# Sketched attention and a squared-ReLU FFN on one core: another flow for one chunk, and a rearranged prologue

## The chip, the cores and the metric

One Trainium2 chip, one of its cores. The metric is the device time of one execution in microseconds (us), the median over several executions; less is better. The engines of the core are TensorE (PE, matrix products; its weight loads are PEld), VectorE (DVE), ScalarE (ACT), GpSimd (POOL) and SyncE (SP, which only issues DMAs). They run side by side, each through its own list of instructions in order, and wait for one another by semaphores. Matrix products are written to PSUM; the other data lies in SBUF.

## The reference

```python
# q, k, v: (4, 4, 1088, 32)  S1, S2: (8, 32)
def phi(x):
    a = np.einsum('rd,bhsd->bhsr', S1, x)
    b = np.einsum('rd,bhsd->bhsr', S2, x)
    return np.einsum('bhsi,bhsj->bhsij', a, b).reshape(*x.shape[:-1], r * r)
q_p, k_p = (phi(q), phi(k))
kv = np.einsum('bhsf,bhsd->bhfd', k_p, v)
z = np.sum(k_p, axis=2)
num = np.einsum('bhsf,bhfd->bhsd', q_p, kv)
den = np.einsum('bhsf,bhf->bhs', q_p, z)[..., None] + 1e-06
x = (num / den)                    # then (batch, token, 4 heads x 32) -> (4352, 128)
h = np.maximum(x @ w_in, 0.0)      # w_in: 128 x 2048
out = h * h @ w_out                # w_out: 2048 x 128
```

Every token's query and key become 64 features (8 by 8 products of two sketches). Attention is linear: keys and values are summed to a 64 x 32 matrix per head (kv) and a vector of 64 (z), and each query's features are multiplied with them. The quotient goes through a feed-forward net with a squared ReLU. All values are 32-bit floats.

## The kernel before

The work is cut into 4 batches, each batch into 3 chunks of 384, 384 and 320 tokens, and the hidden layer of the FFN into 16 blocks of 128 (`NFF`). One block of one chunk is a step, so there are 192 steps. In a step, `ffn1` multiplies a block of `w_in` (cast to 16 bit) with the chunk's `xT` into a PSUM tile `pg` (two buffers); one engine takes the ReLU (`gt`), one the square (`g2`); `ffn2` multiplies it with `w_o` in 32 bit and adds into the chunk's `po`. `ffn1` runs three steps ahead of `ffn2` (`LA = 3`). As an x is brought to a range that suits 16 bit by a power of two or a per-token scale before the FFN, its square (`beta` or `bt`) is multiplied on at the end.

Attention for the chunks to come runs in between. A small planner (`_Plan`) puts each of its pieces into a step: `P.add(key, engine, cost, needs, function)` takes the first step after those of its needs (two steps after for PE, one for the others, unless `lag` says otherwise) in which the engine's planned load stays under a cap (1.2 us for DVE until the first chunk of batch 1, 5.0 for POOL). `ready` demands that a chunk's x is planned two steps before `ffn1` first reads it. `balance` then chooses for every step which engines take ReLU and square. The instructions are written out in this order and each engine follows it.

There are two flows for a query chunk:

- The transposed flow (all chunks but the first two): `a_qg` (PE, L417) makes the sketches of the queries with features on partitions, in the PSUM tile X; `a_sh` (DVE shuffles, L426) spreads them; `a_qpn` (POOL, L435) multiplies; `a_ndn` (PE, L448) multiplies with `kw` into the PSUM tile N; `a_dT`, `a_rd`, `a_rb`, `a_x` (DVE) divide; `a_ax` (ACT) and `a_sum` (PE, L498) find the size; `a_rs`, `a_s2` (DVE, L513, L504) make powers of two; `a_xs` and `a_beta` (POOL, L522, L531) give `xT` and `bt`. Its output goes through `f_sc` and `f_sT`.
- The old flow (chunks 0 and 1 of batch 0): tokens on partitions after `a_nd` (PE, L576); `a_x1`, `a_x2`, `a_x3` (DVE) divide and scale each token; chunk 0 is then transposed by PE (`a_xp`) and copied by ACT (`a_xT`), chunk 1 by a transposing DMA (`a_xd`). `f_br` (POOL, 16 copies) lays out `beta`; the output goes through `f_oT` and `f_ob` (L770).

X and N exist once each, so who fills them next waits for the last reader: kv of the next batch (`a_kv9`, L314) needs N too, which the plan frees at `s2`.

Before the first step lies a prologue, ordered by hand (L832 to L926). S1 and S2 come by two DMAs on ACT's queue into `s_nat`, are transposed on DVE (`s_T`, L229) and copied into three operands: `sk` (keys), `sr` (three blocks, "replicas" of the query sketches) and `sq`/`sqn`. Keys of batch 0 are transposed (`a_kT`), sketched on PE (`a_kf`), copied by ACT (`a_fs`) and multiplied on DVE (`a_kp`), two or three 128-token tiles at a time; `a_kv` and `a_z` sum them on PE. The three replicas of the query sketches (`replicated`, L847) come first for 128 columns, between the kv steps, then for 256 after them; `products` multiplies them. `keep_warm` (L830) gives PE products of zeros where it would otherwise be idle: 10 at the start (`WARM0`) and 3 before the first FFN step (`WARM`). ACT casts both halves of `w_in`. All loads but S1, S2 and two pieces of v go by SP's queue in the order of the code: k, the first 384 columns of q, v, the rest of q, both halves of `w_in`, both of `w_o`.

Of the kernel before, what the change touches and what calls it, by code (L numbers as in the profile page):

```python
# [23 lines left out]
class _Plan:  # L24
# [5 lines left out]
    def __init__(self, nsteps, cap):  # L30
        self.n, self.cap = nsteps, cap
        self.load = {e: [0.0] * nsteps for e in cap}
        self.at, self.slots = {}, [[] for _ in range(nsteps)]
        self.late = []
# [6 lines left out]
    def add(self, key, eng, dur, needs, f, *args, not_in=(), first=0, lag=None):  # L41
        s = first
        for k in needs:
            s = max(s, self.at[k] + (self.LAG[eng] if lag is None else lag))
        while s < self.n - 1 and (
            (self.load[eng][s] > 0 and self.load[eng][s] + dur > self.cap[eng])
            or s % 16 in not_in
        ):
            s += 1
        self.fix(key, eng, dur, s, f, *args)  # L50
        return s
# [3 lines left out]
def kernel(  # L55
# [26 lines left out]
    WARM0, WARM = 10, 3  # L82
# [3 lines left out]
    KG = [[(0, 2), (2, 2), (4, 2), (6, 3)]]  # L86
# [6 lines left out]
    Square = mybir.ActivationFunctionType.Square  # L93
    Copy = mybir.ActivationFunctionType.Copy
# [14 lines left out]
    def load_qk(dst, src, b, c0, c1):  # L109
        nc.sync.dma_start(  # L110
# [34 lines left out]
    for s_, r0 in ((S1, 0), (S2, 8)):  # L145
        nc.scalar.dma_start(s_nat[r0 : r0 + 8, :], s_[:, :])
# [4 lines left out]
    nc.scalar.copy(zero_a[:, :], zero[:, 0:8])  # L151
# [6 lines left out]
    load_v(vn[0], 0, 2, (nc.scalar, nc.scalar))  # L158
    load_v(vn[0], 0, 1)
    load_qk(qn[0], q, 0, 384, S)  # L160
# [4 lines left out]
    for c in range(2):  # L165
        nc.sync.dma_start(
            w_in32[:, 1024 * c : 1024 * c + 1024], moe_w_in[:, 1024 * c : 1024 * c + 1024]
        )
    for c in range(2):
# [8 lines left out]


    sk = cpool.tile([128, 64], F32)  # L180
    sq = cpool.tile([128, 128], F32)
    nc.gpsimd.memset(sk[:], 0.0)
    nc.gpsimd.memset(sq[:], 0.0)
    sr = cpool.tile([128, 3 * 128], F32)
    nc.gpsimd.memset(sr[:], 0.0)
    kT = cpool.tile([128, SP], F32)
    qT = cpool.tile([128, SP], F32)
    nc.gpsimd.memset(kT[:, S:SP], 0.0)
# [7 lines left out]
    nc.gpsimd.memset(part[:], 2.0**-12)  # L196
    tiny = cpool.tile([128, 1], F32)
# [10 lines left out]
    def a_kT(b, part):  # L208
        if b > 0 and part < 2:
# [4 lines left out]
        elif b > 0:  # L214
            nc.vector.transpose(
                _ap(kq, 0, 128, 256, [[32 * NT, 2], [1, 32]]),
                _ap(kn[b], 0, 128, 1024, [[32, 2], [1, 32]]),
            )
        elif part < 2:
            nc.vector.transpose(  # L220
                _ap(kT, 0, 128, 512 * part, [[32, 4], [128, 4], [1, 32]]),
                _ap(kn[b], 0, 128, 512 * part, [[128, 4], [32, 4], [1, 32]]),
            )
        else:
            nc.vector.transpose(kT[:, 1024:S], kn[b][:, 1024:S])
# [4 lines left out]
    for h in range(H):  # L230
        (nc.vector if h < 2 else nc.gpsimd).tensor_copy(
# [3 lines left out]
    for j_, o_, f_, copy in (  # L235
        (2, 8, [[0, 4], [1, 8]], nc.gpsimd.tensor_copy),
        (1, 4, [[1, 4], [0, 8]], nc.scalar.copy),
        (0, 0, [[1, 4], [0, 8]], nc.gpsimd.tensor_copy),
    ):
# [5 lines left out]
    mask_b = [8 + l % 8 for l in range(32)]  # L245
    mask_a = [[4 * e + l // 8 for l in range(32)] for e in range(E)]
# [44 lines left out]
    def a_kp(b, g):  # L291
        t0, n = KG[b][g]
        fs = st[b, "fs", g]
        kp = wpool.tile([128, 5 * 256], F32, tag="kp", name="kp", bufs=4)
# [11 lines left out]
    def a_kv(b, t):  # L306
        if t == 0:
            st[b, "N"] = psa.tile([128, 1024], F32, tag="N", name="kvp")
            st[b, "kvp"] = st[b, "N"]
        kp, at = st[b, "kp", t] if b == 0 else (st[b, "kp2"], kp2_at(t))  # L310
        n = 64 if b == 0 and t == 8 else 128
# [232 lines left out]
    def a_qc(b, ch, pool=psa, tag="feat"):  # L544
        qc = pool.tile([128, 512], F32, tag=tag, name="qc")
        nc.tensor.matmul(qc[:, 0:384], sq[:, :], qT[:, 384 * ch : 384 * ch + 384])
        st[b, "qc", ch] = qc

    def a_qb(b, ch):
        qb = wpool.tile([128, 384], F32, tag="qb", name="qb")  # L550
        nc.vector.stream_shuffle(in_=st[b, "qc", ch][:, 0:384], out=qb[:, :], mask=mask_b)
        st[b, "qb", ch] = qb

    def a_qa(b, ch, e):
        qa = wpool.tile([128, 384], F32, tag="qa", name="qa")
        nc.vector.stream_shuffle(in_=st[b, "qc", ch][:, 0:384], out=qa[:, :], mask=mask_a[e])
        st[b, "qa", ch, e] = qa

    def a_qp(b, ch, e):
        qp = bpool.tile([128, 384], F32, tag="qp", bufs=4, name="qp")  # L560
        nc.vector.tensor_tensor(
            out=qp[:, :], in0=st[b, "qa", ch, e][:, :], in1=st[b, "qb", ch][:, :], op=mult
        )
        st[b, "qp", ch, e] = qp

    def a_nd(b, t):
        ch, o = t // 3, t % 3
        if o == 0:
            if ch == 0:
                st[b, "nd", ch] = st[b, "N"][:, 512:1024]  # L570
            else:
                st[b, "N"] = psa.tile([128, 1024], F32, tag="N", name="nd")
                st[b, "nd", ch] = st[b, "N"]
        nd = st[b, "nd", ch]
        for e in range(E):
            nc.tensor.matmul(  # L576
                nd[:, 132 * o : 132 * o + 132],
                st[b, "qp", ch, e][:, 128 * o : 128 * o + 128],
                st[b, "kvz"][:, 132 * e : 132 * e + 132],
                start=(e == 0),  # L580
                stop=(e == E - 1),
            )


    def nd_ap(b, ch, off, free):
        return _ap(st[b, "N"], 0, 128, (512 if ch == 0 else 0) + off, free)

    def a_x1(b, ch, o=0, n=3):
        def small(tag, m=4):
            return wpool.tile([128, 3 * m], F32, tag=tag, name=tag)  # L590
        if o == 0:
            st[b, "x1", ch] = tuple(small(x) for x in ("den", "rden", "mx"))
        den, rden, mx = (t_[:, 4 * o : 4 * (o + n)] for t_ in st[b, "x1", ch])
        nc.vector.tensor_scalar(
            out=den, in0=nd_ap(b, ch, 132 * o + 32, [[33, 4 * n]]),
            scalar1=1e-6, scalar2=None, op0=add,
        )
        nc.vector.reciprocal(rden, den)
# [3 lines left out]
        )  # L602

    def a_x2(b, ch):
        def small(tag, m=4):
# [3 lines left out]
        mm, mp, rm = (small(x, 1) for x in ("mm", "mp", "rm"))  # L609
        nc.vector.tensor_tensor(out=m1[:, :], in0=mx[:, :], in1=rden[:, :], op=mult)  # L610
# [5 lines left out]
            out=mp[:, :], in0=mm[:, :], scalar1=1.0 / 1024.0, scalar2=1.0 / 1024.0,  # L616
            op0=mult, op1=add,
        )
        nc.vector.reciprocal(rm[:, :], mp[:, :])
        nc.vector.tensor_tensor(  # L620
            out=_ap(sc, 0, 128, 0, [[4, 3], [1, 4]]),
            in0=_ap(rden, 0, 128, 0, [[4, 3], [1, 4]]),
            in1=_ap(rm, 0, 128, 0, [[1, 3], [0, 4]]),
            op=mult,
        )
        st[b, "x2", ch] = sc, mp

    def a_x3(b, ch, o=0, n=3):
# [5 lines left out]
        sc, mp = st[b, "x2", ch]  # L634
# [6 lines left out]
        if o + n == 3:  # L641
            nc.vector.tensor_tensor(  # L642
                out=st[b, "beta"][:, 3 * ch : 3 * ch + 3], in0=mp[:, :], in1=mp[:, :], op=mult,
# [20 lines left out]
    def a_xd(b, ch):  # L664

        nc.sync.dma_start_transpose(
            _ap(st[b, "xT"], 0, 128, 384 * ch, [[128, 3], [1, 128]]), st[b, "xs", ch][:, :]
        )


# [4 lines left out]
    g2s = {}  # L675

    def ffn1(i, on, cols=None):
# [14 lines left out]
        else:  # L692
            nc.vector.tensor_scalar(  # L693
                out=gt[:, c0:c1], in0=pg[:, c0:c1], scalar1=0.0, scalar2=None, op0=amax
            )
        if on[1] == "ACT":
            nc.scalar.activation(g2[:, c0:c1], gt[:, c0:c1], Square)  # L697
# [37 lines left out]
    def f_br(b, ch):  # L735

        if ch == 0:
            st[b, "br"] = bpool.tile([128, 4 * NT], F32, tag="br", name="br")
        for dm in range(4):
# [86 lines left out]
    def keep_warm(n, cols=512):  # L826

        t_ = st["warm"]
        for _ in range(n):
            nc.tensor.matmul(t_[:, 0:cols], zero[:, 0:128], zero[:, 0:cols])  # L830

    st["warm"] = psf.tile([128, 512], F32, tag="pg", name="warm")  # L832
    keep_warm(WARM0)
    a_kf(0, 0, psf, "pg")
# [5 lines left out]
    a_kf(0, 2, psf, "po")  # L840
    a_kf(0, 3, psf, "po")
# [309 lines left out]
```

## Time and profile before

| what | us |
|---|---|
| median of 8 executions | 196.14 |
| lowest, highest | 195.83, 197.29 |
| the profiled execution (one of the eight) | 197.29 |
| its span, first to last instruction | 195.5 |
| first FFN product of the second layer (`po`, L709) starts | 18.56 |
| second layer L709, 386 matmuls, busy | 145.1 |
| first layer L681, 193 matmuls, busy | 61.6 |
| mean granted clock of TensorE | 0.985 |

How to read the profile: each row names the line of the kernel, the engine, the operation, "out<-in" by the names of the tiles, and a shape. An engine's busy time is its own; PE's is modelled, because matmuls overlap. "PEclk" is the share of the full clock that TensorE was granted, a digit for each fortieth of the span. The chain of work that ended last is followed back from the last instruction: at each step to what released it. Each 32-bit product is two matmul instructions.

### The profile page before, as it was taken

Reading aid. Unit: us, or ns where it says so; the run is one execution under the profiler, and the core shown is the slowest. Engines: PE = TensorE matmul, PEld = TensorE weight load, DVE = VectorE, ACT = ScalarE, POOL = GpSimd, SP = SyncE. Lnnn points to the kernel's source line nnn. Section 1 sums busy time; section 2 is a strip of 40 time slices with the busy share of each in tenths; the row PEclk is TensorE's granted clock in tenths of the full one; section 3 lists DMA queues with packets and bytes.
Section 4 is the critical chain, followed back from the end, with each engine's and each line's share of the span. In section 5 each row is a group of like instructions: output and inputs, shape, how many; then the busy total and the mean of one; then the engine's idle time right before and its main releaser. Section 6 shows DMA issues by size and latency. Waiting matters only on the chain.

```text
span 195.5 us, 4446 instructions
## 1 busy us (share of the span) xinstructions
PE 186.9 (96%) x1639; PEld 113.5 (58%) x1639; DVE 131.4 (67%) x326; ACT 141.7 (72%) x322; POOL 97.6 (50%) x162
## 2 busy tenths in 40 slices
PE   7997999989999999999999999999999999999990
PEld 2873665546566555565566554565566555556990
DVE  2966865995596678855676668865766655567740
ACT  3436886985796977877696987867687968767740
POOL 4844526993193756960473656960483942610000
PEclk9999799999999999999999999999999999999997
DMA  6799420020028420020047320020020110110201
GB/s 190 209 277 268 96 84 20 5 32 12 0 37 214 135 34 3 0 45 0 2 60 210 118 33 3 0 44 0 0 44 2 19 19 0 20 21 0 40 3 34
DMA packets 27199, 11.40 MB, mean 58 GB/s; under 512 B 19178, under 2 KB 25770, under 8 KB 27178
## 3 DMA queue, kind: packets, MB, share of 16 engines
q1 hardware_dynamic: 26726, 11.02, 23.0%
q8 instruction: 13, 0.21, 0.5%
q10 hardware_dynamic: 452, 0.10, 0.2%
q14 instruction: 8, 0.07, 0.1%
HBM read 8.78 MB, written 2.23 MB: 56 GB/s over the span
## 4 chain that ended last, share of the span: by engine, by line
PE 88%; DVE 7%; ACT 1%; issue 1%; DVEq 0%
PE po L709 54%; PE pg L681 15%; PE ndn L448 4%; PE kvp L314 3%; PE warm L830 2%; PE pt L726 2%; PE qg L417 1%; PE rep L847 1%; DVE sh L426 1%; PE kf L258 1%; PE kvp L328 1%; PE kf L357 1%; PE kvp L576 1%; DVE ob L770 1%; PE sm L498 1%; PE nd L576 1%
## 5 line engine op out<-in xcount | busy, mean ns | idle before, releaser
L709 PE MATMUL po<-g,w_o 128*128 128x384 f32 (+3 forms) x386 | 145.1, 462 | 0.0
L697 ACT ACTIVATE g<-gt 128x384 f32<-128x384 f32 (+1 forms) x159 | 79.9, 506 | 21.3 <-DVE gt L693 17.6
L709 PEld LDWEIGHTS po<-g,w_o 128*128 128x128 f32 x386 | 66.8, 192 | 32.7 <-issue 22.4
L691 ACT ACTIVATE gt<-pg 128x384 f32<-128x384 f32 (+2 forms) x124 | 56.4, 458 | 14.9 <-PE pg L681 14.2
L681 PE MATMUL pg<-xT,w_in 128*128 128x384 f16 (+2 forms) x193 | 61.6, 320 | 0.6 <-ACT xT L660 0.2
L693 DVE TENSOR_SCALAR gt<-pg 128x384 f32<-128x384 f32 (+1 forms) x69 | 36.7, 532 | 26.5 <-PE pg L681 25.4
L699 POOL TENSOR_TENSOR g<-gt 128x384 f32<-128x384 f32 (+1 forms) x31 | 23.9, 776 | 48.5 <-ACT gt L691 48.2
L681 PEld LDWEIGHTS <-w_in 128*128 128x128 f16 x193 | 19.0, 98 | 24.6 <-issue 7.5
L435 POOL TENSOR_TENSOR qp<-sh 128x384 f32<-128x384 f32 (+1 forms) x20 | 19.2, 964 | 7.3 <-DVE sh L426 5.1
L426 DVE STREAM_SHUFFLE sh<-qg 128x384 f32<-128x384 f32 (+1 forms) x40 | 21.4, 561 | 0.0
L458 DVE STREAM_TRANSPOSE dT<-ndn 128x384 f32<-128x384 f32 (+1 forms) x10 | 5.4, 544 | 11.3 <-PE ndn L448 11.3
L284 POOL TENSOR_TENSOR kp<-fs 128x1152 f32<-128x1152 f32 x3 | 9.5, 3166 | 5.3 <-DVE fs L277 5.3
L522 POOL TENSOR_TENSOR xT<-x,rs 128x384 f16<-128x384 f32 (+1 forms) x10 | 9.5, 949 | 1.7 <-DVE rs L513 1.7
L741 POOL COPY br<-beta 32x3 f32<-32x3 f32 x32 | 6.5, 203 | 5.6 <-DVE beta L642 4.3
L448 PE MATMUL ndn<-qp,kw 64*32 64x192 f32 (+1 forms) x320 | 8.4, 318 | 0.0
L531 POOL TENSOR_TENSOR bt<-s 128x384 f32<-128x384 f32 (+1 forms) x10 | 7.8, 785 | 0.9 <-DVE s L504 0.9
L448 PEld LDWEIGHTS ndn<-qp,kw 64*32 64x32 f32 x320 | 4.7, 106 | 5.2 <-issue 3.8
L340 POOL TENSOR_TENSOR ks<-kp 128x1024 f32<-128x1024 f32 x3 | 7.1, 2370 | 0.2
L513 DVE TENSOR_SCALAR rs<-sm 128x384 uint32<-128x384 uint32 (+1 forms) x10 | 5.2, 521 | 2.5 <-PE sm L498 2.5
L314 PE MATMUL kvp<-kp,vn 128*32 128x64 f32 (+1 forms) x288 | 5.9, 221 | 0.7 <-DVE s L504 0.7
L351 POOL TENSOR_TENSOR ks<-ks 128x512 f32<-128x512 f32 (+1 forms) x6 | 6.2, 1035 | 0.5
L314 PEld LDWEIGHTS kvp<-kp,vn 128*32 128x32 f32 (+1 forms) x288 | 4.7, 109 | 2.8 <-DVE s L504 1.3
(119 smaller groups left out, 157.4 us busy)
## 6 DMA issues: line engine op xcount, KB each, us to landing
vn<-in_v_dram SPq DMA_DIRECT2D x32, 64.0 KB, 3.9
kn<-in_k_dram SPq DMA_DIRECT2D x3, 544.0 KB, 12.2
qn<-in_q_dram SPq DMA_DIRECT2D x3, 544.0 KB, 3.3
out_dram<-oT SPq DMA_DIRECT2D x24, 48.0 KB, 1.9
w_in<-in_moe_w_in_dram SPq DMA_DIRECT2D x2, 512.0 KB, 5.3
w_o<-in_moe_w_out_dram SPq DMA_DIRECT2D x2, 512.0 KB, 11.0
out_dram<-oT SPq DMA_DIRECT2D x12, 40.0 KB, 1.7
out_dram<-ob SPq DMA_DIRECT2D x8, 48.0 KB, 1.9
```

The source lines that it names most:

```text
L284: (nc.vector if g == 0 else nc.gpsimd).tensor_tensor(out=_ap(st[b, "kp2"], 0, 128, 128 * NT * g, [[64, 2 * NT], [8, 8], [1, 8]]), in0=_ap( ...
L314: nc.tensor.matmul(st[b, "kvp"][32 * h : 32 * h + 32, 0:64], _ap(vn[b], 0, n, v0 + dv * h, [[1, 32]]), kp[0:n, at[h] : at[h] + 64], start= ...
L426: nc.vector.stream_shuffle(in_=_ap(st[b, "qg", ch], 0, 128, 0, [[512, 2], [1, n]]), out=_ap(t_, 0, 128, 0, [[n, 2], [1, n]]), mask=mask_q[ ...
L435: nc.gpsimd.tensor_tensor(out=qp[:, 0 : 2 * n], in0=st[b, "sh", ch, s, 0][:, 0 : 2 * n], in1=st[b, "sh", ch, s, 1][:, 0 : 2 * n], op=mult,)
L448: nc.tensor.matmul(nd[32 * h : 32 * h + 32, 512 * g + 192 * i : 512 * g + 192 * i + n], st[b, "kw"][64 * g : 64 * g + 64, 128 * i + 32 * h ...
L522: nc.gpsimd.tensor_tensor(out=st[b, "xT"][:, 384 * ch : 384 * ch + n], in0=st[b, "x", ch][:, 0:n], in1=st[b, "rs", ch][:, 0:n], op=mult,)
L681: nc.tensor.matmul(pg[:, c0:c1], w_in[:, 128 * c : 128 * c + 128], st[b, "xT"][:, 384 * ch + c0 : 384 * ch + c1],)
L691: nc.scalar.activation(gt[:, c0:c1], pg[:, c0:c1], Relu)
L693: nc.vector.tensor_scalar(out=gt[:, c0:c1], in0=pg[:, c0:c1], scalar1=0.0, scalar2=None, op0=amax)
L697: nc.scalar.activation(g2[:, c0:c1], gt[:, c0:c1], Square)
L699: (nc.vector if on[1] == "DVE" else nc.gpsimd).tensor_tensor(out=g2[:, c0:c1], in0=gt[:, c0:c1], in1=gt[:, c0:c1], op=mult)
L709: nc.tensor.matmul(st["po", b, ch][:, c0:c1], w_o[:, 128 * c : 128 * c + 128], g2s[i][1][:, c0:c1], start=first, stop=(c == NFF - 1), skip ...
```

## The change

It moves chunk 1 of batch 0 to the transposed flow and rearranges the prologue:

- `old_chunk` and its helpers (`a_qc`, `a_qb`, `a_qa`, `a_qp`, `a_nd`, `a_xd`) go. Chunk 1 of batch 0 now runs through `feature_tasks`, `nd_tasks` and `x_tasks`; its sketches `a_qg(0, 1)`, the transposes `a_kvT(0)` and the copy `a_kw(0)` stand in the prologue, the first two while DVE works on the token scale of chunk 0.
- S2 is loaded by a DMA on GpSimd's queue, before its memsets. The v pieces of ACT's queue go to SP. q comes in three pieces, `w_in` and `w_o` in alternating halves.
- Key tiles 4 to 8 are sketched by eight products with features on partitions (`kf4`), turned by one DVE transpose (`fs4`), and multiplied in two parts. The kv sums of batch 0 lie in a `po` buffer.
- Replicas are made for all 384 columns: blocks 2 and 0 before all kv steps, block 1 after them.
- In `a_x1` the `den` of chunk 0 goes to ACT; `a_x2` uses a power of two by bit operations, one DVE instruction less. `beta` needs one more after xs.
- The second half of `w_in` is cast by POOL in two pieces. Four of the 16 `f_br` copies of chunk 0 stay ahead of the steps, twelve are planned.
- Two of the four `sk` copies go from POOL to ACT. `WARM0` is 8 and a half one, `WARM` 5.
- A square on ACT is written after the next step's ReLU (`square_due`), except in the last chunk.
- The planner treats POOL as one sequence of work with measured lengths; the costs of `balance` are computed from widths.

```diff
+        if eng == "POOL":
+            d, t = dur / 0.85, float(s)
+            for t0, t1 in sorted(self.pool):
+                if t + d <= t0:
+                    break
+                t = max(t, t1)
+            self.pool.append((t, t + d))
+            s = int(t)
+            self.fix(key, eng, dur, s, f, *args)
+            self.at[key] = max(s, int(t + d - 0.6))
+            return s
...
-    for s_, r0 in ((S1, 0), (S2, 8)):
-        nc.scalar.dma_start(s_nat[r0 : r0 + 8, :], s_[:, :])
+    nc.gpsimd.dma_start(s_nat[8:16, :], S2[:, :])
+    nc.scalar.dma_start(s_nat[0:8, :], S1[:, :])
...
+    load_qk(qn[0], q, 0, 384, 768)
+    load_w_in(0, nc.sync)
+    load_w_o(0)
+    load_qk(qn[0], q, 0, 768, S)
+    load_w_in(1, nc.sync)
+    load_w_o(1)
...
-        (nc.vector if h < 2 else nc.gpsimd).tensor_copy(
+        (nc.vector.tensor_copy if h < 2 else nc.scalar.copy)(
...
+        if ch == 0:
+            nc.scalar.activation(
+                den, nd_ap(b, ch, 132 * o + 32, [[33, 4 * n]]), Iden, bias=eps[:, 0:1]
+            )
...
+    def square_due():
+        while due:
+            dst, src = due.pop()
+            nc.scalar.activation(dst, src, Square)
...
+        square_due()
         if on[1] == "ACT":
-            nc.scalar.activation(g2[:, c0:c1], gt[:, c0:c1], Square)
+            due.append((g2[:, c0:c1], gt[:, c0:c1]))
+            if i >= NS - NFF:
+                square_due()
...
-    a_kf(0, 2, psf, "po")
-    a_kf(0, 3, psf, "po")
+    a_sr(1, nc.scalar.copy)
+    kf4 = psa.tile([128, 1024], F32, tag="N", name="kf")
+    for g in range(2):
+        for p0 in range(4):
+            nc.tensor.matmul(
+                kf4[32 * p0 : 32 * p0 + 32, 512 * g : 512 * g + 160],
+                sk[64 * g : 64 * g + 64, 32 * g : 32 * g + 32],
+                kq[64 * g : 64 * g + 64, 32 * NT * p0 + 128 : 32 * NT * p0 + 288],
+            )
     a_qT(0, 0, 384)
...
-    replicated(2, 0, 128, psf, "pg")
+    replicated(2, psf.tile([128, 512], F32, tag="pg", name="rep"))
+    x0 = psa.tile([128, 1024], F32, tag="X", name="rep")
+    replicated(0, x0[:, 0:512])
     a_kp(0, 0)
     a_kp(0, 1)
+    fs4 = wpool.tile([128, 320], F32, tag="fs", name="fs")
+    nc.vector.transpose(
+        _ap(fs4, 0, 128, 0, [[32, 2], [64, 5], [1, 32]]),
+        _ap(kf4, 0, 128, 0, [[512, 2], [32, 5], [1, 32]]),
+    )
+    kp4 = wpool.tile([128, 5 * 256], F32, tag="kp", name="kp", bufs=3)
+    for lo, n in ((0, 2), (2, 3)):
+        nc.vector.tensor_tensor(
...
-    nc.scalar.copy(qb[:, 0:128], rep[2, 0][:, 0:128])
-    products(0, 128)
-    replicated(2, 128, 384, psf, "pg")
-    replicated(0, 128, 384, psf, "po")
-    replicated(1, 128, 384, psf, "po")
+    nc.scalar.copy(qb[:, :], rep[2][:, 0:384])
+    products(0)
+    replicated(1, x0[:, 512:1024])
     a_kvz(0)
-    nc.scalar.copy(qb[:, 128:384], rep[2, 128][:, 0:256])
-    products(128, 384)
+    products(1)
+    a_qT(0, 384, 768)
     a_kvs(0)
...
+    a_kvT(0)
+    a_qg(0, 1)
     st["warm"] = psf.tile([128, 512], F32, tag="pg", name="warm")
     keep_warm(WARM)
     a_x1(0, 0)
+    w_cast(0, 1024, nc.scalar.copy)
     a_x2(0, 0)
...
     a_xT(0, 0, 1, 2)
-    a_qb(0, 1)
-    f_br(0, 0)
+    a_kw(0)
...
-    old_chunk()
+    P.at["kw", 0] = -1
+    feature_tasks(0, 1)
+    P.add(("qT", 0, 2), "DVE", 0.45, [], a_qT, 0, 768, S)
+    f_br(0, 0, 0, 1)
+    for i in range(2):
+        P.add(("w", i), "POOL", 0.6, [], w_cast, 1024 + 512 * i, 512, nc.gpsimd.tensor_copy)
+    assert P.at["w", 1] < 5
+    P.add(("br", 0, 0), "POOL", 2.6, [], f_br, 0, 0, 1, 4)
+    nd_tasks(0, 1)
+    x_tasks(0, 1)
     feature_tasks(0, 2)
```

## The prediction

> **What bounds the kernel now.** I read the page first, then the chain of work that ended last in order of time, then the waits of PE, then PE's timeline step by step, and last the one-microsecond windows of the start. The page:
>
> ```profile
> span 195.5 us, 4446 instructions
> PE 186.9 (96%) x1639; PEld 113.5 (58%) x1639; DVE 131.4 (67%) x326; ACT 141.7 (72%) x322; POOL 97.6 (50%) x162
> PEclk9999799999999999999999999999999999999997
> PE 88%; DVE 7%; ACT 1%; issue 1%; DVEq 0%
> ```
>
> PE is the bound, and 88% of the chain is PE. Only what shortens PE's work, lets it start earlier or removes a stall can count. The chain shows where PE was not the one waited for:
>
> ```profile
> 10.92 1.49 PE rep L847 x6
> 12.42 1.50 PE kvp L576 x12
> 15.93 0.62 DVE xs L635 x2
> 17.07 0.55 ACT xT L660 x2
> 18.72 1.36 PE po L709 x4
> ...
> 36.11 1.15 DVE de L467
> ...
> 39.91 1.47 DVE ob L770
> ...
> 43.73 1.21 PE kvp L314 x72
> 45.44 0.65 PE po L709 x2
> ```
>
> Up to 18.6 us a serial prologue runs. From 45.3 us on, the chain is PE without a break: the second product's start-to-start is 0.81 us for 384 columns and 0.67 us for 320, plus PE's own attention tasks. Between lies one weak place, 39.4 to 45.3 us. PE's timeline there (start, duration):
>
> ```profile
> 39.35 0.81 PE L709 MATMUL po<-g,w_o 128*128 128x384 f32 x2
> 40.33 0.81 PE L709 MATMUL po<-g,w_o 128*128 128x384 f32 x2
> 41.26 0.81 PE L709 MATMUL po<-g,w_o 128*128 128x384 f32 x2
> 42.20 0.81 PE L709 MATMUL po<-g,w_o 128*128 128x384 f32 x2
> 45.27 0.81 PE L709 MATMUL po<-g,w_o 128*128 128x384 f32 x2
> ```
>
> Two steps take 0.93 and 0.94 us, and the last gap is 3.07 us, where the same gap (kv of the next batch inside) is 2.28 us at 85.28 and at 129.19. So 2 x 0.125 + 0.79 = 1.04 us is stall. Its cause:
>
> ```profile
> PE kvp L314 <- DVE s L504: 0.7, 1, 0.7
> ```
>
> kv of batch 1 waits for the accumulator N, which VectorE's s2 of chunk (0,2) frees late. The start has a second loss (columns: busy time of each engine, then PEclk):
>
> ```profile
> 16.00:17.00 1.00, 0.19 (x3) 0.28 (x4) 1.00 (x5) 0.00 (x0) 0.28 (x2) 1.00 1.05 335
> 19.00:20.00 1.00, 1.00 (x3) 0.63 (x4) 0.22 (x1) 0.75 (x2) 0.84 (x5) 0.50 0.84 158
> ```
>
> PE is nearly idle at 16 us, and about 3.4 us of half clock follow (18.8 to 22.2 us). The first three steps take 1.95, 1.60 and 0.86 us, 4.41 against 3 x 0.81 = 2.42: 1.99 us lost to clock and start-up together.
>
> **What the skill says.** The Trainium skill, "TensorE: Matmul & The Clock Gate", Part 1, says the array clock is halved after a window of about 3.4 us with too little work, and that the windows run free of the kernel. The 3.4 us at 0.50 agree; the threshold is not shown here. "SBUF — State Buffer", section Who interferes with whom, says GpSimd and VectorE lock each other out of a shared port pair. The trace agrees: `de` on ten elements takes 1.14 us at 36.11 beside a 3.12 us GpSimd product, against 0.17 us for `den` on twelve at 14.02. "DMA: Bandwidth & Descriptors", Specifications, gives about 1 us to the first byte from the GpSimd queue and 0.6 us from the others; no GpSimd DMA is in this trace.
>
> **The change, prologue.** S2 alone on the GpSimd queue: by the trace both S transfers have landed at 4.27 us, and `s_T` starts at 4.40, just after the kT transpose (3.59 + 0.71 = 4.30). Above, the gain is at most 0.1 us. Below, if the GpSimd transfer lands at 5.3, everything after it moves 1 us. Issued at about 0.95 (after the memset of `s_nat`), with the page's 1 us to the first byte and the 0.9 us from first packet to landing that S1 shows (2.53 to 3.47), it lands at an estimated 2.9, so 1.4 us of slack: I take 0. The GpSimd memsets queued behind it (1.9 us, 0.74 to 2.65) then end near 4, before `s_T`.
>
> The key path. VectorE does transposes and the first two kp to about 7.55 (start-to-start 0.61 for 512 elements, first at 6.3). New there is the fs4 transpose (0.45 us; fs L277 of 288 elements has 0.43) in place of four ScalarE copies, then kp4 in parts of 512 and 768: done at 7.55 + 0.45 + 0.61 + 0.94 = 9.55, where the last kp ended at 9.08. On PE two full replicas (0.64 us each) stand before kv. The second needs GpSimd's sr block 0, at about 7.0 (two sk copies, 0.43 us, leave the queue ahead of the eight sr copies that ended at 8.28, and four of these eight no longer precede block 0 under VectorE's lock). So kv starts at 7.8, not 7.66. That 0.15 us is covered by kp4, which kv 6 to 8 wait for; without that cover it would be 0.15 to 0.7. kv 6 to 8 run at 9.62, 9.84 and 10.06, and `kvt` can start at 10.56 rather than 10.99: 0.43 us earlier.
>
> After kv, before has six replica matmuls (1.49 us) before `nd`; now one replica (0.64), with the first product on VectorE already done. kvz ends at 11.41, `nd` runs 11.5 to 12.95 (12 matmuls, 1.34 us to the last start), and the token scale can start at 13.1 rather than 14.02: 0.92. Its own chain loses two VectorE instructions: `den` goes to ScalarE beside the reduce and `mp` goes, at about 0.2 us each (14.02, 14.23; 15.31, 15.51). xs then starts at 14.6 rather than 15.93: 1.3 us. The kv transposes, qg and five warm-up matmuls (0.22 us each) fill PE meanwhile to about 14.7; qc (0.88) and its shuffle are gone.
>
> On ScalarE the kw copy (0.37 us) now stands between xT and the first relu: minus 0.3. So po starts at 17.5 rather than 18.56. The second step hangs on a ScalarE square that moves behind relu 2 and ends 0.66 us earlier than its 19.36. I take 0.85 as the mean; ends 0 and 1.3.
>
> **The loop.** Removed from PE in batch 0: nd of chunk 1 (0.90 + 0.45 in steps at 22.97 and 24.68) and kvT (0.21) = 1.56. Added: ndn with qg (2.02 - 0.81 = 1.21, the step at 49.53) and the sum (0.17) = 1.38. Gain 0.18. Removed from VectorE for this chunk: two qa, two qp, x1 to x3, about 5 us; added about as much (four sh, dT, rd, rb, x, rs, s2). The chunk's transposing DMA, SP's wait for it and GpSimd's sixteen br copies (3.56 us) go; GpSimd gets two products, xs, bt and two weight casts.
>
> The plan by hand: sh in steps 0 and 1, nd in 4, sum in 9, rs in 10, xs in 11; it is due when step 13 opens. From the sum to that opening are 3 x 0.81 = 2.43 us, for sum, rs (0.5), xs (0.95) and three hops of about 0.15: slack about 0.4. Kv of batch 1 moves from step 22 to about 30, by which time N (s2 in step 23) is long free, so the 0.79 us goes. The two ScalarE-bound steps also go: a relu and its own square are 0.50 apart and the next relu 0.43 later (37.33, 37.83, 38.26); with the square one step late both spacings can be 0.43, 0.86 a step for 0.93. Of 1.04 I take back 0.84 and leave 0.2 for new waits, which next would come at chunk 1's xs. Later steps have no stall to lose, and their PE tasks are the same; the new costs of the planner count 0 there.
>
> **Sum.** 0.85 + 0.18 + 0.84 = 1.87 us. The profiled execution took 197.29 us (195.5 span and 1.8 around it) and would take 195.4. It is 1.15 us above the median of 196.14; how much of that is the half-clock window is not shown. Against the median: 194.3.
>
> **Rivals.** (1) The half clock goes too: the gap before the first ffn matmul is filled by two more warm-ups and less waiting. Against it, about 2.5 us of thin work between 15 and 17.5 remain, as now. Of the 1.99 us start-up loss about 1.4 would go: 192.9. (2) The front gives nothing, because S2 or a replica is late (1 us), and a new wait takes the old stall's place: only 0.2 is left, 195.9. For it: an unseen queue, and kv behind two replicas. Against: each has cover above. (3) Slower: chunk 1 starves PE at step 13. Its chain, from shuffles to xs, alternates VectorE, GpSimd, PE and ScalarE in 11 steps; the old one had until a transposing DMA at 28.54 landed about 31, with 2.7 us to spare. Each VectorE instruction caught behind GpSimd costs about 1 us (`de` 1.14, `ob` 1.64 at 39.80), and GpSimd waits in its queue for the second half of w_in before the products. From 2.5 us over the slack it decides; three such blocks and no slack give 2.7: 197.0. Against: hand start-to-starts put xs at about 29 us, PE's need at about 30.
>
> **Numbers.** 194.3 has chance 0.66, with its own range 193.5 to 195.4; rival 1 0.12, rival 2 0.10, rival 3 0.12. Counting 0.3% (0.6 us) as what a measurement tells from none: faster 0.78, same 0.10, slower 0.12. The range, 192.9 to 196.1, leaves rival 3 and the far edges out.
>
> **What would show it.** First po near 17.5 us and xs near 14.6; kvt near 10.6; `s_T` still at 4.4; kv of batch 1 without a wait on s2; no PE gap at the first matmul of chunk 1; the loop's later steps at 0.81 and 0.67 as now. I am wrong if `s_T` starts after 5, if PE waits on xT (0,1) for over a microsecond, or if ScalarE sets the first twelve steps.

## The result, and the profile after

The changed kernel took 197.23 us (median of 20 executions, 195.5 to 199.12) beside 195.9 us for the kernel before (57 executions): slower by 1.3 us, where 194.3 us was forecast. The ratio is 1.0033 with the interval [1.0013, 1.0053]; ratios here leave out executions more than 1.5% above the fastest of the same kernel, medians count them all. Executions of the changed kernel stand in three groups, near 195.5, 197.1 and 199.1 us, while those of before lie between 195.4 and 196.6 us with five exceptions. The execution profiled before (197.29 us) was such an exception, with a half-clock window at 18.8 us; the one profiled after took 199.16 us.

The page of after (span, busy time of PE, shares of the chain):

```profile
span 197.4 us, 4576 instructions
...
PE 188.0 (95%) x1675; PEld 111.7 (57%) x1675; DVE 121.4 (62%) x303; ACT 139.4 (71%) x342; POOL 96.3 (49%) x144
...
PE 86%; DVE 7%; ACT 2%; DMA 2%; issue 1%; DVEq 0%; ACTq 0%
```

VectorE has ten microseconds less to do than before, and PE is the bound as it was. New in the chain's shares is DMA. The chain of after in order of time (start, length, what):

```profile
1.25 3.45 DMA s_nat<-in_S_dram
5.61 1.94 PE kf L276 x8
7.55 0.71 PE kf L839 x16
8.27 2.86 PE rep L849 x4
15.43 1.59 PE nd L910 x12
...
40.56 2.57 DVE ob L764
...
52.03 1.14 PE kvp L334 x72
```

Three things are to be seen. S2's transfer, issued on the GpSimd queue at 1.25 us, opens the chain. Two replicas, forecast at 0.64 us each, hold PE from 8.27 to 11.1 us, and `nd` starts at 15.43 us instead of the forecast 11.5. And a stall by `ob` stands at 40.56 us, where the stall before kv of batch 1 has gone: that group starts at 51.96 us right behind its step, and its gap between two second products is 2.25 us (51.22 to 53.47), as at the later batches.

PE's timeline of after tells why the front is late (start, busy time of the group, idle before it and its releaser in brackets):

```profile
1.23 3.81 PE L824 MATMUL warm<-zero 128*128 128x512 f16 x9 [1.23 <-DVE zero L161]
5.61 1.94 PE L276 MATMUL kf<-sk,kT 128*128 128x64 f32 x8 [0.57 <-ACT sk L251]
...
12.98 0.44 PE L348 MATMUL kvp<-kp,ones 128*32 128x64 f32 x8
13.19 0.38 PE L334 MATMUL kvp<-kp,vn 128*32 128x64 f32 x8
13.40 0.28 PE L348 MATMUL kvp<-kp,ones 128*32 128x64 f32 x8
13.51 0.28 PE L334 MATMUL kvp<-kp,vn 128*32 128x64 f32 x8
```

The same groups of eight start 0.21 us apart up to 13.4 us and 0.11 us apart after it: PE ran at half clock until then. The throttle's first record in this trace is full clock from 13.38 us; ahead of that record the PEclk column shows 1.00, which is no reading. In the trace of before, whose first warm-ups take 0.43 us each for 0.22 later on, that record is at 5.14 us. So after stays at half clock for 8.2 us more, with its front up to the kv sums in them, behind a gap of 0.57 us that before does not have. PE's timeline of before at that place:

```profile
1.23 4.25 PE L830 MATMUL warm<-zero 128*128 128x512 f16 x10 [1.23 <-DVE zero L149]
5.31 2.14 PE L258 MATMUL kf<-sk,kT 128*128 128x64 f32 x18
```

The stall at 40 us, from after's list of PE's waits and the timelines of VectorE and GpSimd:

```profile
PE sm L518 <- ACT ax L513: 0.7, 1, 0.7
```

```profile
40.34 0.22 DVE L491 RECIPROCAL rd<-de 128x10 f32<-128x10 f32 x1
40.48 2.65 DVE L764 TENSOR_TENSOR ob<-oT,br 128x384 f32<-128x384 f32 x1
43.05 0.50 DVE L496 STREAM_TRANSPOSE rb<-rd 128x320 f32<-128x320 f32 x1
43.59 0.49 DVE L503 TENSOR_TENSOR x<-ndn,rb 128x320 f32<-128x320 f32 x1
```

```profile
40.36 2.36 POOL L360 TENSOR_TENSOR ks<-kp 128x1024 f32<-128x1024 f32 x1
```

GpSimd's `ks1` starts 0.12 us ahead of `ob` and runs to 42.72 us; `ob`, two inputs from SBUF, takes 2.65 us. The token scale of chunk (0,2), which hangs behind it in VectorE's queue (`rb`, `x`, then `ax` on ScalarE), is late, and the sum that PE has next waits.

### The profile page after: what moved, and what is told of

It is laid out like the page before. It is cut to its first block, busy times and chain, and to the rows that moved or that the text cites. A ratio compares the mean times of both kernels' runs of the same rounds, so it can differ in the third digit from the quotient of the medians.

```text
span 197.4 us, 4576 instructions
## 1 busy us (share of the span) xinstructions
PE 188.0 (95%) x1675; PEld 111.7 (57%) x1675; DVE 121.4 (62%) x303; ACT 139.4 (71%) x342; POOL 96.3 (49%) x144
## 4 chain that ended last, share of the span: by engine, by line
PE 86%; DVE 7%; ACT 2%; DMA 2%; issue 1%; DVEq 0%; ACTq 0%
PE po L703 54%; PE pg L672 14%; PE ndn L468 4%; PE kvp L334 3%; PE pt L720 2%; DMA s_nat<-in_S_dram 2%; PE qg L437 2%; PE rep L849 1%; DVE ob L764 1%; PE kvp L348 1%; PE kf L276 1%; PE nd L910 1%; PE sm L518 1%; PE kf L377 1%; ACT g L666 1%
## 5 line engine op out<-in xcount | busy, mean ns | idle before, releaser
L682 ACT ACTIVATE gt<-pg 128x384 f32<-128x384 f32 (+2 forms) x143 | 67.3, 475 | 28.3 <-PE pg L672 27.6
L703 PEld LDWEIGHTS po<-g,w_o 128*128 128x128 f32 x386 | 65.8, 190 | 33.8 <-ACT g L666 19.3
L684 DVE TENSOR_SCALAR gt<-pg 128x384 f32<-128x384 f32 (+1 forms) x50 | 26.1, 523 | 30.9 <-PE pg L672 24.3
L693 POOL TENSOR_TENSOR g<-gt 128x320 f32<-128x320 f32 (+1 forms) x28 | 21.5, 774 | 45.5 <-ACT gt L682 45.4
L455 POOL TENSOR_TENSOR qp<-sh 128x384 f32<-128x384 f32 (+1 forms) x22 | 20.9, 952 | 12.0 <-DVE sh L446 12.0
L446 DVE STREAM_SHUFFLE sh<-qg 128x384 f32<-128x384 f32 (+1 forms) x44 | 22.4, 565 | 0.0
L735 POOL COPY br<-beta 32x3 f32<-32x3 f32 x16 | 2.9, 183 | 9.6 <-DMA vn<-in_v_dram 8.9
L513 ACT ACTIVATE ax<-x,tiny 128x384 bf16<-128x384 f32 (+1 forms) x11 | 6.5, 590 | 1.3 <-DVE x L503 1.3
L749 DVE SCALAR_TENSOR_TENSOR sc<-po,bt 128x384 f32<-128x384 f32 (+1 forms) x10 | 5.3, 532 | 3.3 <-PE po L703 3.1
L334 PEld LDWEIGHTS kvp<-kp,vn 128*32 128x32 f32 x288 | 5.4, 120 | 2.7 <-issue 1.6
```

Of the source, the lines that this page charges most:

```text
L334: nc.tensor.matmul(st[b, "kvp"][32 * h : 32 * h + 32, 0:64], _ap(vn[b], 0, n, v0 + dv * h, [[1, 32]]), kp[0:n, at[h] : at[h] + 64], start= ...
L446: nc.vector.stream_shuffle(in_=_ap(st[b, "qg", ch], 0, 128, 0, [[512, 2], [1, n]]), out=_ap(t_, 0, 128, 0, [[n, 2], [1, n]]), mask=mask_q[ ...
L455: nc.gpsimd.tensor_tensor(out=qp[:, 0 : 2 * n], in0=st[b, "sh", ch, s, 0][:, 0 : 2 * n], in1=st[b, "sh", ch, s, 1][:, 0 : 2 * n], op=mult,)
L682: nc.scalar.activation(gt[:, c0:c1], pg[:, c0:c1], Relu)
L684: nc.vector.tensor_scalar(out=gt[:, c0:c1], in0=pg[:, c0:c1], scalar1=0.0, scalar2=None, op0=amax)
L693: (nc.vector if on[1] == "DVE" else nc.gpsimd).tensor_tensor(out=g2[:, c0:c1], in0=gt[:, c0:c1], in1=gt[:, c0:c1], op=mult)
```

## The experiments

Theory A was: S2 lands late, PE idles before the key sketches, and the half clock lasts longer. B: the new order of the prologue is itself slower or brings the groups of times. C: new stalls in the loop. After the first four runs A split into theory W (too little PE work ahead of the key sketches, the count of warm-ups) and the price of S2 itself. Ratios are to the kernel before, on the same chip. The last column counts from 196.7 us because the changed kernel's groups part there; in e7 and e9 to e15, whose fastest executions take 193.3 to 194.2 us, it counts only those some 2.5 us or more above the fastest.

| kernel | median us (executions) | ratio, interval | at 196.7 us or over |
|---|---|---|---|
| e1 change again | 197.25 (20) | 1.0030 [1.0004, 1.0056] | 15 |
| e2 change, S2 on ScalarE's queue | 196.97 (22) | 1.0023 [1.0003, 1.0042] | 15 |
| e3 change, ten warm-ups | 196.22 (22) | 1.0022 [1.0007, 1.0037] | 7 |
| e4 before, S2 on GpSimd's queue | 196.13 (22) | 1.0018 [1.0009, 1.0027] | 1 |
| e5 before, eight warm-ups | 199.33 (4) | 1.0163 [1.0131, 1.0195] | 4 |
| e6 start repaired (e2 and e3) | 196.03 (22) | 1.0002 [0.9983, 1.0021] | 5 |
| e7 e6, `ob` two steps later | 194.75 (13) | 0.9935 [0.9914, 0.9957] | 0 |
| e8 e6, `den` on VectorE, transposes moved | 198.04 (17) | 1.0051 [1.0022, 1.0081] | 14 |
| e9 e7, three warm-ups before the scale | 194.84 (10) | 0.9944 [0.9912, 0.9975] | 0 |
| e10 e7, first warm-ups split | 195.25 (22) | 0.9954 [0.9932, 0.9975] | 7 |
| e11 e7, `den` on VectorE, own tile | 193.88 (6) | 0.9903 [0.9869, 0.9937] | 0 |
| e12 e9 and e11 | 194.08 (19) | 0.9920 [0.9896, 0.9945] | 0 |
| e13 e11, S2 on GpSimd's queue | 194.98 (14) | 0.9939 [0.9917, 0.9961] | 1 |
| e14 e11, eight warm-ups | 194.22 (13) | 0.9919 [0.9894, 0.9944] | 3 |
| e15 e11 again | 194.44 (8) | 0.9936 [0.9905, 0.9967] | 0 |

Before stood at 195.73 (e1 to e4, 3 of 73 executions at 196.7 or over), 195.83 (e5 to e8, 2 of 45), 195.84 (e9 to e12, 4 of 44) and 195.92 us (e13 to e15, 1 of 28).

### The start: S2 and the warm-ups (e1 to e6)

e1 is the changed kernel unedited.

> The changed kernel once more, for a profile in another phase of the clock's windows. Theory A (S2 lands late from the GpSimd queue, PE idles before the key sketches, and the half clock then lasts one or two windows of 3.4 us longer): times at separate levels near 195.6, 197.2 and 199, and where the level is low, PE is at full clock from about 5 us on. Theory B (the new order of the prologue is slow by itself): the low level too has its first po later than 18 us. Theory C (new stalls in the loop): a stall of over 1 us near chunk 2 of batch 0 in every profile.

```diff
-    nc.gpsimd.dma_start(s_nat[8:16, :], S2[:, :])
     nc.scalar.dma_start(s_nat[0:8, :], S1[:, :])
+    nc.scalar.dma_start(s_nat[8:16, :], S2[:, :])
```

> The changed kernel with S2 back on ScalarE's queue behind S1. Theory A: s_T starts at 4.4 instead of 4.8 us, PE's idle gap before the key sketches shrinks from 0.57 to under 0.2 us, the levels at 197 and 199 go, median 195.0 to 195.4. Theory B or C: the levels stay and the median moves by less than 0.3 us.

```diff
-    WARM0, WARM = 8, 5
+    WARM0, WARM = 10, 5
```

> The changed kernel with 10.5 instead of 8.5 warm-up products ahead of the key sketches. Theory A: s_T still starts at 4.8, but PE has no gap and the level at 199 goes; the lowest time is that of the changed kernel or up to 0.3 us more, the median about 1 us below it. Theory B or C: no difference beyond 0.3 us.

e4 is the kernel before with S2 issued by `nc.gpsimd` ahead of S1, as the change has it.

> The kernel before with S2 alone moved to the GpSimd queue. Theory A: s_T starts at about 4.8 instead of 4.4 us, the key sketches 0.35 us later, PE's gap before them stays under 0.3 us because ten warm-up products end at 5.5, so the time grows by 0.3 to 0.5 us and the level at 199 is rare. Theory B or C: no change over 0.2 us.

e1 repeated the loss and the stall by `ob` (2.65 us at 40.45 us), as C expected. Its profile fell into the group near 199 us, so what A and B say of the lowest group was not seen in it. e2 kept the groups of times, and PE's gap is 0.31 us where under 0.2 was expected (0.30 in e1), so S2's queue does not make the groups, and A as it stood fell.

What the groups are can be read from the throttle's records. Within each trace the changes of the clock lie multiples of 3.41 us apart; one such window at half clock costs a busy PE up to 1.7 us, which is about the spacing of the groups. The execution of after (199.16 us) comes to full clock at 13.38 us and keeps it; that of e1 (199.16 us too) comes to it at 10.09 us and falls back once, from 20.33 to 23.74 us.

With ten warm-ups (e3) PE has no gap before the first key sketch; its timeline of e3:

```profile
1.23 4.66 PE L824 MATMUL warm<-zero 128*128 128x512 f16 x11 [1.23 <-DVE zero L161]
5.68 1.12 PE L276 MATMUL kf<-sk,kT 128*128 128x64 f32 x8
```

The key sketches start 0.07 us later than in after (5.61 us) and take 1.12 us for 1.94; full clock holds from 5.92 us, and the first matmul of the first product starts at 16.80 us instead of 20.11. The median falls by 1.0 us against e1; two executions near 199 us and over are left. e4 prices S2 alone: 0.4 us more than before, `s_T` at 4.62 us instead of 4.40. The number of warm-ups was then taken by itself, in the kernel before:

```diff
-    WARM0, WARM = 10, 3
+    WARM0, WARM = 8, 3
```

> Kernel before with eight warm-up matmuls of 512 columns ahead of the key sketches instead of ten, nothing else. Theory W (too little work in TensorE's first window lets the half clock last longer): PE stands idle some 0.4 us before the first key sketch, some executions fall on levels about 1.5 and 3.5 us higher, as those of the changed kernel do, and the median rises by 0.3 to 1.5 us; in a profile the full clock starts later than 5.1 us or a half-clock window stands later. Rival B (the new order of the prologue itself brings the levels): before stays at 195.7 with nearly all runs within 0.6 us.

PE's timeline of e5:

```profile
1.23 3.60 PE L830 MATMUL warm<-zero 128*128 128x512 f16 x8 [1.23 <-DVE zero L149]
5.36 3.04 PE L258 MATMUL kf<-sk,kT 128*128 128x64 f32 x13 [0.53 <-POOL sk L231]
```

Two warm-ups fewer cost the kernel before 3.5 us, in all four executions: a gap of 0.53 us, key sketches of 3.04 us, and full clock only from 13.89 us, as in after. The new order of the prologue is not needed for that; W holds, and the loss was larger than it expected.

e6 joins the edits of e2 and e3.

> Changed kernel with ten warm-ups and S2 back on the ScalarE queue. Theory W: the levels vanish, all runs within 0.7 us, median near 195.5 (before less 0 to 0.4): the stall in the loop (1.4 us) still eats what the prologue gained. Rival B: the levels of 197 and 199 stay in a third of the runs or more.

The group near 199 us is gone and the change is even with before. W's median (195.5) and spread (0.7 us) were missed: 196.03 us, from 195.27 to 197.26. Five executions remain at 196.7 to 197.3: the profiled one has a half-clock window from 18.26 to 21.68 us, as the one of before had, behind PE's thin stretch before the first product.

### The loop: `ob` behind `ks1` (e7)

```diff
     where = balance()
+    late_ob = next(t_ for t_ in P.slots[18] if t_[0] is f_ob)
+    P.slots[18].remove(late_ob)
+    P.slots[20].append(late_ob)
```

> As the start-repaired kernel, and chunk 0's last product and its store are issued two steps later (step 20 in place of 18), after the token scale of chunk (0,2), with everything else in its place. Theory L (GpSimd's ks1 holds the shared port, the product waits behind it and holds up the sum that PE needs): the 1.4 us gap of PE before that sum goes, and the time falls by 1.0 to 1.4 us against the start-repaired kernel. Rival: the sum waits for its own chain or kv of batch 1 takes the wait over; gain under 0.3 us.

Timelines of e7: VectorE, GpSimd beside its `ob`, then PE:

```profile
37.88 0.22 DVE L491 RECIPROCAL rd<-de 128x10 f32<-128x10 f32 x1
38.13 0.51 DVE L496 STREAM_TRANSPOSE rb<-rd 128x320 f32<-128x320 f32 x1
38.68 0.49 DVE L503 TENSOR_TENSOR x<-ndn,rb 128x320 f32<-128x320 f32 x1
...
40.57 1.18 DVE L764 TENSOR_TENSOR ob<-oT,br 128x384 f32<-128x384 f32 x1
```

```profile
40.34 1.00 POOL L455 TENSOR_TENSOR qp<-sh 128x384 f32<-128x384 f32 x1
```

```profile
40.75 0.81 PE L703 MATMUL po<-g,w_o 128*128 128x384 f32 x2
41.40 0.30 PE L518 MATMUL sm<-ax,part 128*128 128x320 bf16 x1
41.53 0.33 PE L672 MATMUL pg<-xT,w_in 128*128 128x384 f16 x1
41.70 0.81 PE L703 MATMUL po<-g,w_o 128*128 128x384 f32 x2
```

`rb` follows `rd` by 0.25 us instead of 2.71, and the sum runs between two steps without a wait; the step that holds it takes 0.95 us instead of 2.30 (after: 43.22 to 45.52 us). The time falls by 1.28 us against e6, the ratio from 1.0002 to 0.9935, with intervals apart: the place of `ob` made the stall, at the size that theory L expected. That GpSimd is what holds `ob` was not varied by itself, but the times fit it closely: `ob` ends 0.41 us after the GpSimd product that it overlaps, in after (42.72 and 43.13 us), in e6 (40.69, 41.10) and in e7 (41.34, 41.75), though that product takes 2.36 us in the first two and 1.00 us in the last. In e7 PE has no wait that leads back to `ob`.

### The denominator on ScalarE (e8, e11)

What e6 shows of `den` and the reduce (ScalarE's timeline, then VectorE's):

```profile
13.64 0.27 ACT L574 ACTIVATE den<-nd,eps 128x12 f32<-128x12 f32 x1 [2.19 <-PE nd L416]
```

```profile
13.95 0.56 DVE L582 TENSOR_REDUCE mx<-nd 128x12 f32<-128x384 f32 x1 [1.36 <-ACT den L574]
```

`den` waits for L416, the kv transposes that write the same PSUM tile, and `mx` waits for `den`. The Trainium skill, "PSUM — Partial Sum Buffer", section Terms, says that two engines may not be on one PSUM bank and quadrant at once, reads included; both read `nd` there, and the trace shows them one after the other.

```diff
-        if ch == 0:
+        if ch < 0:
             nc.scalar.activation(
...
-    a_kvT(0)
     a_qg(0, 1)
...
     a_x1(0, 0)
+    a_kvT(0)
```

> As the start-repaired kernel, with the denominator of chunk 0 back on VectorE and the transposes of kv emitted behind it. Theory S (ScalarE's denominator does not run beside VectorE's reduce: the reduce waits for it, and it waits for the kv transposes): xs starts 0.3 to 0.6 us earlier than with the start repaired alone, and the time falls by as much. Rival: the reduce is held by nd itself, so xs does not move or moves later by the 0.2 us of the added VectorE instruction.

The edit was badly placed. VectorE's timeline of e8:

```profile
14.67 0.17 DVE L605 SCALAR_TENSOR_TENSOR sc<-rden,rm 128x12 f32<-128x12 f32 x1
16.47 0.62 DVE L620 TENSOR_TENSOR xs<-nd,sc 128x128 f16<-128x128 f32 x2 [1.64 <-PE nd L416]
```

The scale was ready 0.61 us earlier than in e6 (15.28; `nd` itself was 0.10 earlier), but xs then waited 1.64 us for the transposes, which now wrote the tile ahead of it. They came late because PE stood for 1.11 us before them without a releaser ("issue", treated below); another 0.39 us followed behind them, a half-clock window followed at 18.11 us, and 14 of 17 executions stood at 196.7 us or over. e11 gives the transposes a tile of their own instead and leaves them in place, on the base of e7:

```diff
-                st[b, "N"][:, 512 + 128 * i : 640 + 128 * i],
+                st["kvT"][:, 128 * i : 128 * i + 128],
...
+        if b == 0:
+            st["kvT"] = psf.tile([128, 512], F32, tag="po", name="kvT")[:, 0:256]
```

> As the kernel with the late product, with the denominator of chunk 0 on VectorE and the kv transposes in a PSUM tile of their own, in their old place on PE. Theory S (the tile shared with the transposes and the ScalarE denominator hold the reduce): den starts 0.3 us earlier than before, mx 0.5 us, xs 0.4 us earlier counted from kvz; if PE then waits for instructions, xp moves less, 0 to 0.3 us. Rival: xs does not move.

VectorE's timeline of e11, then PE's:

```profile
13.43 0.17 DVE L582 TENSOR_SCALAR den<-nd 128x12 f32<-128x12 f32 x1 [0.77 <-PE nd L914]
13.52 0.55 DVE L586 TENSOR_REDUCE mx<-nd 128x12 f32<-128x384 f32 x1
...
15.05 0.62 DVE L624 TENSOR_TENSOR xs<-nd,sc 128x128 f16<-128x128 f32 x2
```

```profile
15.47 0.59 PE L828 MATMUL warm<-zero 128*128 128x512 f16 x2 [0.61 <-issue]
15.90 0.49 PE L646 MATMUL xp<-iden,xs 128*128 128x128 f16 x3
```

From `kvz` to xs it is 3.82 us (11.23 to 15.05) instead of 4.33 in e6 (11.15 to 15.48): theory S holds, with 0.5 us where 0.4 was expected. e11 moves `den` and gives the transposes their own tile at once; which of the two gives the 0.5 us is not separated. In time, 193.88 us stands beside 194.75 of e7 on another chip, and the intervals overlap; so do those of e9 and e12, which differ by the same edit on one chip (194.84 and 194.08 us). e15, e11's kernel again, gave 194.44. What the 0.5 us is worth in time is therefore not settled, and PE's lines say why it need not show: xp did not start at xs.

### PE without instructions (e9, e10, e12)

In e6, e7 and e11 PE stands for 0.6 to 1.5 us after the third warm-up, and the profile names no releaser ("issue"). In e7 a 16 KB packet of the queue of kind instruction starts at 14.61 us and takes 0.96 us; PE goes on at 16.86, when xs (16.11, 0.62 us) is done. Theory I is that PE had used up what was fetched.

```diff
-    WARM0, WARM = 10, 5
+    WARM0, WARM = 10, 3
```

> As the kernel with the late product (start repaired), with three warm-up matmuls before the token scale instead of five. Theory I (PE runs out of fetched instructions there: a 16 KB packet of its instruction queue starts near 13.4 us, and PE stands without a wait until some 1.4 us after it has come): PE issues the same number of instructions before it stands, so the idle stretch now ends in xp itself, at the moment at which the fourth warm-up ran, and xp starts 0.2 to 0.4 us earlier; time 0 to 0.4 us less. Rival (the fourth warm-up waits for its PSUM buffer or another event, not for instructions): no idle put down to issue is left, xp starts 0.3 us after xs.

```diff
-    keep_warm(WARM0)
+    keep_warm(2 * WARM0, 256)
```

> As the kernel with the late product, with the ten first warm-ups of 512 columns as twenty of 256: the same columns, twenty PE instructions more. Theory I: the idle stretch put down to issue comes about twenty instructions earlier, in the key-value transposes or qg before the third warm-up, and its packet starts some tenths of a microsecond earlier; den, mx and xs move only if the transposes are held. Rival (a hidden event): the stretch stays behind the third warm-up.

PE's timeline of e9, then of e10:

```profile
17.21 0.33 PE L642 MATMUL xp<-iden,xs 128*128 128x128 f16 x3 [1.73 <-DVE beta L632]
```

```profile
13.54 0.53 PE L437 MATMUL qg<-qT,sqn 64*32 64x192 f32 x9
14.31 0.53 PE L437 MATMUL qg<-qT,sqn 64*32 64x192 f32 x7 [0.24 <-issue]
14.76 1.25 PE L824 MATMUL warm<-zero 128*128 128x512 f16 x5
15.90 0.61 PE L642 MATMUL xp<-iden,xs 128*128 128x128 f16 x3
```

In e9 the idle stretch ends in xp, 1.42 us after the packet has come (14.77 + 1.02 = 15.79 us), where e7 has 1.29 and e11 1.54; the releaser that the profile names, `beta`, is inferred, and xs was done 0.4 us earlier. In e10 twenty instructions more ahead of it move the stretch out of the warm-ups into the middle of qg, and its packet to 11.81 us. A hidden event of the warm-ups would have stayed with them. The other traces agree: in e3 and in e6 to e15, eleven in all, the stretch comes after the 218th matmul of the trace, whichever that is, and PE goes on 1.29 to 1.58 us after the packet has come. In e8 this put it ahead of the transposes. The Trainium skill, "Runtime: NRT & Kernel Launch", section Instruction fetch mechanics, says that an engine's instructions are refilled in blocks of 16 KiB by its own DMA queue, and that the cost is mostly hidden; the packet size agrees, and in this prologue of small matmuls beside full DMA engines it was not hidden. No gain in time shows in e9 (194.84 us, on another chip than e7's 194.75; from `kvz` to xp 0.17 us less in the trace). e10 has single executions up to 200.17 us; why the split warm-ups bring these was not tried.

> The last two together: three warm-ups, denominator on VectorE, transposes in a tile of their own, with start repaired and product late. Theories I and S: xp is set by the instruction fetch alone, 0.2 to 0.6 us earlier than with the late product; time 194.2 to 194.7, under both kernels, unless less PE work before xp lets the half clock in again, which would show as times 1 to 2 us higher in some executions.

e12 is e11 with the three warm-ups of e9. Its xp starts at 16.29 us, 1.47 us after the packet, with xs starting at 15.56: now set by the fetch alone, as expected. The 194.08 us lie just under the expected 194.2 to 194.7, and are no better than e11.

### The two start edits again, on the best kernel (e13 to e15)

> As the kernel with the denominator on VectorE and late product (193.9 us), with S2 alone back on the GpSimd queue. If S2 lands late and the key sketches wait: first key sketch 0.1 to 0.4 us later and the time up by the same, 194.0 to 194.3. Rival: S2 also opens a gap ahead of the key sketches that brings the half clock in; then single executions stand 1 to 3 us higher.

> As the kernel with the denominator on VectorE and late product, with eight first warm-ups alone instead of ten. Theory W: PE idle 0.3 us or more before the first key sketch, the full clock starts one or two windows of 3.4 us later in many executions, median up by 1 to 3.5 us, 195 to 197.5. Rival: no change, since S2's late landing made that gap, not the two warm-ups.

> The kernel with the denominator on VectorE, the transposes in a tile of their own, the product late and the start repaired, once more: 193.9 us, ratio near 0.990, all executions within 1.5 us.

e13 is e11 with S2 back on GpSimd's queue: `s_T` at 4.90 us instead of 4.47 (e15), first key sketch at 5.72 instead of 5.49, median 0.5 us higher. The sign is that of e4, though the two intervals overlap. e14 is e11 with eight warm-ups:

```profile
1.23 3.81 PE L828 MATMUL warm<-zero 128*128 128x512 f16 x9 [1.23 <-DVE zero L161]
5.30 1.24 PE L276 MATMUL kf<-sk,kT 128*128 128x64 f32 x8 [0.26 <-ACT sk L251]
```

The gap is 0.26 us, 3 of 13 executions stand at 196.7 to 197.2 us (none of 8 in e15), but the median is not raised: W's expectation of 195 to 197.5 failed there. The length of the gap alone does not decide. It is 0.57 us in after and 0.30 us in e1, the same kernel, with 14 and 15 of 20 executions at 196.7 us or over; 0.31 us in e2 with 15 of 22, and 0.53 us in e5 with all four. e14 also ran on another chip than these.

The traces suggest what does decide, as an estimate that no run tested. Counted at 0.43 us for a warm-up product at half clock (their spacing in e3) and 0.11 us for a key-sketch matmul (a sixth of the 0.64 us between 384-column replica matmuls in after), PE works in 82 to 100% of the last 3.41 us before the full clock in 13 traces: those with ten warm-ups, and e14. In after, e1, e2 and e5, the windows that took in the end of the eight warm-ups and the first key sketches are filled to 53 to 69%, and full clock came one or more windows later. In e14 the window happened to end at 5.64 us, with little of the gap and the sketches in it; in e1, e2 and after it ended at 6.42 to 6.68 us. On this reading eight warm-ups are enough only where the grid of windows lies well, and ten were enough up to 6.72 us (e9).

## Why the prediction was wrong

**Warm-ups: a cost that was left out.** The reduction of the first warm-ups from ten to eight was not priced at all; the text counted only the five later ones, which "fill PE". Rival 1 even let the half clock go. It stays longer instead: 3.3 us of front in the profiled execution (first ffn matmul at 20.11 us, 16.80 with ten), 1.0 us of the median (e3), and 3.5 us in the kernel before (e5). The trace showed what was at stake: in before, the ten warm-ups end just where the key sketches begin.

**S2: "I take 0".** The estimate of 2.9 us for its landing missed by 1.8 us: 4.71 us in after. The transfer was issued at 1.25 us instead of 0.95; its first packet started at 3.38 us, 2.13 us after the issue (2.13 to 2.39 in the five traces with that queue), where 1 us was taken; and it landed 1.33 us after that, where 0.9 was taken. `s_T` starts at 4.51 to 4.90 us in these five and at 4.39 to 4.53 in the twelve without, and 0.4 us of time go (e4), between the stated ends of 0.1 gained and 1 lost. The Trainium skill, "DMA: Bandwidth & Descriptors", section Anatomy of one DMA, gives some 2.0 us as the fixed time of a GpSimd transfer, setup and completion together; the 1.9 us of the prediction was near that, and the 3.46 us from issue to landing here are not.

**The key path.** With the start repaired, `kvt` stands at 10.73 us (10.56 forecast) and `nd` at 11.73 (11.5) in e6: this reasoning held within 0.25 us there, where full clock came at 4.61 us. In e7 it came at 6.41 us, and both stand 0.6 us later.

**`den` "beside the reduce".** It runs ahead of it. Of the 0.4 us by which the token-scale chain was to be shorter, nothing came: from the start of `nd` to xs it is 3.75 us in e6 (11.73 to 15.48) for 3.64 in the profile of before (12.29 to 15.93). With `den` on VectorE and the transposes apart it is 3.24 (11.81 to 15.05 in e11); xs was forecast at 14.6, and the first po, at 17.75 us there, at 17.5.

**The loop: "I take back 0.84 and leave 0.2 for new waits".** The old stall went as described, chunk 1 came in time (rival 3 fell: no gap at its first matmul), and the two ScalarE-bound steps of 0.93 us run at 0.81. The term for new waits was mis-sized, by the medians the largest miss (1.28 us, e6 to e7): one new wait of 1.3 us, at the sum of chunk (0,2) and not at chunk 1's xs. The text had the very case in its hands, `ob` of 1.64 us at 39.80, but saw it as a danger to chunk 1 alone. From the fourth to the 57th matmul of the first product, undisturbed by half clock, e4 takes 49.49 us, e3 49.93 and e7 48.37: the loop was to give 1.02 us (0.18 + 0.84), lost 0.44 with `ob` in its place, and gives 1.12 with `ob` late.

**The sum.** 1.87 us was forecast. With the four faults mended (e11, e15) the kernel runs 1.96 and 1.48 us under before, at 193.9 and 194.4 us: about that gain was there to be had, but in a kernel with four edits that the prediction does not have. By number rival 3 (197.0) came nearest, by luck: chunk 1 did not starve PE. In kind it was rival 2, a late S2 with a new wait, whose 195.9 us left out the clock. None of the three signs of being wrong appeared; neither the warm-ups nor `ob` before the sum of chunk (0,2) was among them.

The version of e11 beats both kernels; to before its ratio is 0.9903 [0.9869, 0.9937] and again 0.9936 [0.9905, 0.9967].

## What to carry to other kernels

Count what keeps TensorE busy up to its first real matmul, and price a removed warm-up at whole half-clock windows (up to 1.7 us each here), not at its own 0.4 us. Before placing a VectorE instruction with two SBUF inputs ahead of a chain that feeds PE, look at what GpSimd starts at that moment. Do not count two engines that read one PSUM tile as parallel lines: in e6 they formed a chain, and the transposes into that tile joined it.

## What the runs showed that was not expected

PE can stand for instructions: 0.24 to 1.5 us in a prologue of small matmuls, until 1.3 to 1.6 us after a 16 KB packet of the instruction queue has arrived (14.61 + 0.96, going on at 16.86 us in e7). Where it stands follows the count of instructions ahead of it (after 218 matmuls in eleven traces), not the work. And two warm-ups fewer, which left 0.5 us of idle ahead of the key sketches, kept the half clock on for some 8 us more (13.89 us in e5, 5.14 in before).
